# Alternating two sequences in a fused retention and feed-forward kernel, and attending two tiles in one stop

## The chip, the cores and the metric

The kernel runs on one core of a Trainium2 chip. Its time is the device time of one execution in microseconds (us); the lower, the better. The engines of the core work side by side, each on its own list of instructions in order: TensorE (PE in the profile, its weight loads PEld), VectorE (DVE), ScalarE (ACT), GpSimd (POOL) and SyncE (SP). Transfers are issued here by SyncE and GpSimd and carried out by 16 DMA engines.

## The reference

A retention layer is followed by a feed-forward layer. There are 4 sequences (batch), 8 heads, 768 tokens and 64 values a head.

```python
gamma = 1.0 - 2.0 ** (-5.0 - np.arange(H))
scale = 1.0 / np.sqrt(D)
for t in range(S):                       # attention: a decaying state for each head
    state = gamma * state + outer(k[:, :, t], v[:, :, t])
    y[:, :, t] = scale * q[:, :, t] @ state
x = y.transpose(0, 2, 1, 3).reshape(B * S, H * D)      # 3072 tokens x 512
h = x @ w_in                                           # 512 -> 2048
s = np.sin(alpha * h)
out = (h + s * s / (alpha + 1e-09)) @ w_out            # 2048 -> 512
```

## The kernel before

**Tiles and groups.** A sequence is cut into 6 chunks of 128 tokens; a chunk is a tile, numbered `j = 6 * sequence + chunk`, so there are 24. The list `order` (also `P`) is the order in which they are worked on: first chunk 0 of each of the four sequences (`e0` to `e3`), then chunks 1 to 5 of sequence 0, of sequence 1, and so on. The tiles of `order` are put together in ten groups: 4 tiles in group 0, 2 each in groups 1 to 8, 4 in group 9.

**Attention of a tile** is done in chunks: a masked product of q and k inside the tile (`scores`, then the mask on VectorE into `aT`), its product with v, the product of q with the state that earlier chunks left (`inter`, from `s_q`), and the addition of the tile's own k and v product to the state (`sums`; VectorE adds it to `s_f` in `keep`, and `hand` copies `s_f` to a bf16 `s_q`). The decay is taken into v (multiplied by `kg` or `kgq` in `scale_v`) and into the result (`leave`, which multiplies by `qg` into `xT`). One call of `burst(old, new)` makes one stop on TensorE: `inter` and the rest of the old tile, and the scores of the new one, so that VectorE can mask these until the next stop. `behind(last)` makes TensorE wait until the matmul `last` has written.

A tile has one of two forms. A *narrow* tile is loaded by itself (`load_chunk`: q and k into `qkr`, v into `vr`; for tiles in `spread`, q and k in two transfers each) and needs 16 score matmuls of 128 columns and a mask over 1024 columns. A *wide* tile (`wide(j)`) is laid out with half of its tokens on each half of the partitions, so that the upper right quarter of the scores isn't worked out: 768 columns. Wide tiles are loaded a whole sequence at a time (`load_seq`: for each of q, k, v eight transfers, one a head, each with all chunks of that head). Before, the wide ones are chunks 3 to 5 of sequence 1 and chunks 1 to 5 of sequences 2 and 3.

**Transposes.** q and k are needed with the head's values on the partitions (`qkT`). For the first tiles TensorE transposes; from `order[8]` on `turn(j)` has SyncE issue a DMA transpose (L278) two stops ahead. It waits for the loads of q and k, and what stands behind it on SyncE's list, output stores among it, waits with it.

**Feed-forward.** A phase `g` works on group `g` slot by slot: `Slot` makes the first product (L515, 8 matmuls into one bank of `ph`), ScalarE takes sine and square (L518, L523), VectorE combines both in `add` (L530) into `gT`. After each slot's matmuls stand the output matmuls (L540) of the group before, 4 in each slot of groups 2 to 8 when these have 8 slots. A stop stands behind the slot's first product: slot (g, n) is slot n of phase g.

**Where stops stand.** The stops of the two tiles of group g + 1 stand in slots 1 and 5 of phase g; the four of group 9 in slots 0, 2, 4 and 6 of phase 8. The order on every engine is that of the program, written out by hand (`manual_schedule`); waits come from the data alone.

**PSUM** has eight banks: four of tag `mm` (`ph`, output tiles `po` and others), two of `two` (`py`, the old tile's result) and two of `pa` (the new tile's scores, with the state sums of a wide tile in columns 384 to 512).

**Loads.** GpSimd issues nearly all loads, since they change float to bf16, in the order of the program, and between them it multiplies v by the decay (L158), which waits for that v. Its list behind the first tiles reads: chunk loads up to `order[10]`, then q, k, v of sequence 1, of sequence 2, of sequence 3, with products of v in between.

Of the kernel before, what the change touches and what calls it, by code (L numbers as in the profile page):

```python
# [16 lines left out]
def kernel(  # L17
# [31 lines left out]
    order += [b * NCH + c for b in range(B) for c in range(1, NCH)]  # L49
# [18 lines left out]
    raw = {}  # L68

# [8 lines left out]
    def spread(j):  # L78

        return j in order[8:11]  # L80
# [21 lines left out]

    def wide(j):
        return j >= NCH + 3 and j % NCH > 0
# [38 lines left out]
    wake = consts.tile([32, 256], F32, name="wake")  # L143
    nc.sync.dma_start(out=wake, in_=w_in_v[0:32, 0, 0:256])
    alpha_row = consts.tile([FF, 128], F32, name="alpha_row")
# [8 lines left out]
    def scale_v(j, eng):  # L154
        t, by = raw["v", j], kg
        if wide(j):
            t, by = t.rearrange("i f p d -> i (f p) d"), kgq
        eng.tensor_mul(t, t, by[:, j % NCH, :, None].to_broadcast([128, H, D]))  # L158
# [83 lines left out]
    s_f = big.tile([128, NP, D], F32, name="s_f")  # L242
    s_q = [big.tile([128, NP, D], BF16, name=f"s_q{i}") for i in range(2)]
# [3 lines left out]
    xT = {}  # L247

# [32 lines left out]
    def stage_A(j, parts=1):  # L281
# [7 lines left out]
        aT = st["aT", j] = work.tile([128, 2, NP, 128], BF16, name="aT", tag="aT", bufs=2)  # L289
# [8 lines left out]
    def first_state(j):  # L298

        ps = psum.tile([128, NP, D], F32, name="ps", tag="mm", bufs=4)  # L300
        for b, m, e in heads:
            h = head(b, m, e)
            nc.tensor.matmul(ps[half(e), 2 * b + m, :], raw["k", j][:, h, :], raw["v", j][:, h, :],
                             start=(b == 0 and m == 0), stop=True, skip_group_check=True)

        def copies():
            nc.scalar.copy(s_q[1], ps)
            nc.vector.tensor_copy(s_f, ps)
        return copies
# [27 lines left out]
    def inter(j, apart):  # L337

        qkT, s = st["qkT", j], s_q[j % NCH % 2]
# [16 lines left out]
    def scores(j):  # L356

        qkT = st["qkT", j]
        pa = st["pa", j] = psum.tile([128, 2, 512], F32, name="pa", tag="pa")
        if not wide(j):  # L360
# [4 lines left out]
            aT = st["aT", j] = work.tile([128, 2, NP, 128], BF16, name="aT", tag="aT", bufs=2)  # L365
            return {"mask": lambda: nc.vector.tensor_mul(aT.rearrange("p e n t -> p (e n) t"),  # L366
                                                         pa.rearrange("p e (n t) -> p (e n) t", n=NP), mask_bc)}
        for m in range(2):
            for b, e in tiles4:
                nc.tensor.matmul(pa[half(b), e, 192 * m:192 * m + 128].rearrange("p (f i) -> p f i", f=2),  # L370
                                 qkT[half(e), 2 + m, half(b)], qkT[half(e), m:m + 5:4, half(b)],
                                 start=(m == 0), stop=True, skip_group_check=True)
            for b, e in tiles4:
                nc.tensor.matmul(pa[half(b), e, 192 * m + 128:192 * m + 192],
                                 qkT[half(e), 6 + m, half(b)], qkT[half(e), 4 + m, half(b)],
                                 start=False, stop=True, skip_group_check=True)
        aT = st["aT", j] = work.tile([128, 2, 2, 192], BF16, name="aTw", tag="aT", bufs=2)
        return {"mask": lambda: nc.vector.tensor_mul(aT, pa[:, :, 0:384].rearrange("p e (m t) -> p e m t", m=2),  # L378
                                                     maskq[:, None, None, :].to_broadcast([128, 2, 2, 192]))}

    def sums(now, to, lo, rs=(0, 1)):

        ks, vs = raw["k", now], raw["v", now]
        for r in rs:
            for b, m, e in heads:
                if wide(now):
                    bank, at, kh, vh = b, lo, ks[half(b), r, 2 * m + e, :], vs[half(b), r, 2 * m + e, :]
                else:
                    h, f = head(b, m, e), b ^ r
                    bank, at, vh = f, lo, vs[half(f), h, :]  # L390
                    kh = ks[half(f), h, :]
                last = nc.tensor.matmul(to[bank][half(e), at + 64 * m:at + 64 * m + 64], kh, vh,  # L392
                                        start=False, stop=True, skip_group_check=True)
        return last
# [6 lines left out]
    def mix(j, tiles):  # L401

        py, aT, vs = st["py", j], st["aT", j], raw["v", j]
        for m in range(2):
            for f in range(2):
                for b, e in tiles:
# [238 lines left out]
    def phase(g, outs, att, nf=1, on_vector=()):  # L645
# [3 lines left out]
        for n in range(FF // nf):  # L649
# [6 lines left out]
            if fresh:  # L656
                rest[0] = fresh
# [179 lines left out]
```

## Time and profile before

| | before |
|---|---|
| time of the runs, median of 3 | 209.84 us (209.36 to 212.28) |
| span of the profiled execution, first to last instruction | 207.7 us |
| granted TensorE clock, mean | 1.000 |
| PE busy | 197.8 us, 95% |
| DVE busy | 151.8 us, 73% |
| ACT busy | 152.5 us, 73% |
| POOL busy | 117.6 us, 57% |
| bytes moved by DMA | 24.79 MB in 102634 packets, 93088 of them under 512 bytes |

The span is the profiled execution's own time between its first and its last instruction; the time of a run has some microseconds around it, here 2.1 between the median and the span. Busy times of one engine can be compared with the span, but not added over engines. In the rows of a timeline the first number is the start in us from the beginning of the span, the second the length. Matmuls are pipelined, so two that follow each other can overlap in these rows. "x8" is a count of instructions that the row merges, and brackets hold the idle time of the engine before it and what ended it. A name such as L515 is a line of the kernel.

### The profile page before, as it was taken

What the parts mean: (1) busy time and instruction counts of PE and PEld (TensorE: products, weight loads), DVE (VectorE), ACT (ScalarE), POOL (GpSimd) and SP (SyncE); (2) the same over time, 40 slices, a digit from 0 to 9 for tenths busy, and PEclk for the clock granted to TensorE, in tenths of its full rate; (3) what the DMA queues carried; (4) which work ended last, traced back from release to release, by engine and by line L of the source; (5) the groups of instructions that cost most, each with busy time, mean ns of one, the idle gap of its engine ahead of it and who ended that gap; (6) DMA issues with size and microseconds to landing.
All of it is one profiled execution on the core that took longest, in us unless ns stands there. A gap on an engine that the chain in (4) does not pass through costs nothing.

```text
span 207.7 us, 5741 instructions
## 1 busy us (share of the span) xinstructions
PE 197.8 (95%) x2339; PEld 123.2 (59%) x2367; DVE 151.8 (73%) x315; ACT 152.5 (73%) x311; POOL 117.6 (57%) x159
## 2 busy tenths in 40 slices
PE   7789999999999999999999999999999999999994
PEld 3345544467766676666666666666666654444453
DVE  5777498677999987868878868868888965656220
ACT  7769788457997787687687687687686779998001
POOL 8999975899999999997599910002022300000000
DMA  8999999999999999999999994421421101010212
GB/s 131 153 176 194 200 197 172 167 181 188 151 124 161 141 207 143 173 103 171 170 146 146 160 146 44 104 72 33 106 68 36 54 2 52 0 51 3 101 51 101
DMA packets 102634, 24.79 MB, mean 119 GB/s; under 512 B 93088, under 2 KB 99664, under 8 KB 102608
## 3 DMA queue, kind: packets, MB, share of 16 engines
q0 software_dynamic: 79808, 13.38, 92.2%
q1 hardware_dynamic: 22656, 10.99, 24.9%
q8 instruction: 18, 0.29, 0.6%
q10 hardware_dynamic: 144, 0.07, 0.1%
q14 instruction: 8, 0.07, 0.1%
HBM read 27.30 MB, written 6.29 MB: 162 GB/s over the span
## 4 chain that ended last, share of the span: by engine, by line
PE 83%; POOL 6%; DMA 3%; ACT 3%; issue 2%; DVE 1%; POOLq 0%
PE po L540 37%; PE ph L515 37%; DMA w_out<-in_moe_w_out_dram 3%; POOL qkr L100 3%; PE py L353 2%; POOL vr L100 2%; PE poh L565 2%; ACT s L518 2%; PE py L407 1%; ACT s L523 1%; PE pt L269 1%; PE pa L370 1%; POOL w_in L131 1%; PE pa L363 1%; PE pa L392 1%
## 5 line engine op out<-in xcount | busy, mean ns | idle before, releaser
L530 DVE SCALAR_TENSOR_TENSOR gT<-s,rec_alpha,ph 128x256 bf16<-128x256 f32 (+3 forms) x164 | 79.9, 523 | 31.5 <-ACT s L523 31.2
L515 PE MATMUL ph<-xT,w_in 128*128 128x256 bf16 (+3 forms) x652 | 98.4, 290 | 0.8 <-issue 0.3
L518 ACT ACTIVATE s<-ph,alpha_sb 128x256 f32<-128x256 f32 (+3 forms) x164 | 76.1, 507 | 27.3 <-PE ph L515 27.2
L540 PE MATMUL po<-w_out,gT 128*128 128x512 bf16 x345 | 90.7, 379 | 2.8 <-issue 2.4
L515 PEld LDWEIGHTS <-w_in 128*128 128x128 bf16 x656 | 63.3, 98 | 33.6 <-issue 0.9
L523 ACT ACTIVATE s<-s 128x512 f32<-128x512 f32 (+1 forms) x94 | 58.8, 625 | 3.0
L540 PEld LDWEIGHTS <-gT 128*128 128x128 bf16 x368 | 34.0, 98 | 30.2 <-DVE gT L530 0.5
L486 POOL CAST s_q<-s_f 128x256 bf16<-128x256 f32 x5 | 2.0, 397 | 35.5 <-DVE s_f L471 19.1
L552 DVE COPY o_sb<-po 128x512 f32<-128x512 f32 x20 | 13.8, 690 | 10.3 <-PE po L540 9.8
L120 POOL DMA_DIRECT2D qk_seq<-in_q_dram x24 | 17.0, 756 | 4.0 <-DMA v_seq<-in_v_dram 4.0
L120 POOL DMA_DIRECT2D qk_seq<-in_k_dram x24 | 16.8, 739 | 0.1
L120 POOL DMA_DIRECT2D v_seq<-in_v_dram x24 | 16.8, 752 | 0.0
L158 POOL TENSOR_TENSOR v_seq<-v_seq,kgq 128x512 bf16<-128x512 bf16 x13 | 13.6, 1071 | 4.3 <-DMA v_seq<-in_v_dram 4.3
L460 DVE TENSOR_TENSOR xT<-py,qg 128x512 bf16<-128x512 f32 x19 | 13.0, 684 | 0.6 <-PE py L423 0.6
L378 DVE TENSOR_TENSOR aTw<-pa,maskq 128x768 bf16<-128x768 f32 x13 | 12.4, 952 | 0.0
L100 POOL DMA_DIRECT2D vr<-in_v_dram x11 | 10.2, 928 | 1.0 <-DMA w_in<-in_moe_w_in_dram 0.6
L569 ACT COPY o_sb<-poh 128x256 f32<-128x256 f32 (+1 forms) x2 | 0.6, 320 | 11.7 <-PE poh L565 11.2
L585 PE MATMUL spare<-warm 128*128 128x512 bf16 x21 | 7.5, 485 | 1.2 <-DVE warm L181 1.2
L366 DVE TENSOR_TENSOR aT<-pa,mask 128x1024 bf16<-128x1024 f32 x7 | 8.5, 1219 | 0.2 <-PE pa L363 0.2
L486 ACT CAST s_q<-s_f 128x256 bf16<-128x256 f32 x14 | 5.5, 392 | 3.1 <-DVE s_f L480 2.6
L100 POOL DMA_DIRECT2D qkr<-in_k_dram x7 | 6.3, 895 | 2.2 <-DMA qkr<-in_q_dram 1.1
L100 POOL DMA_DIRECT2D qkr<-in_q_dram x7 | 6.4, 920 | 0.4 <-DMA w_out<-in_moe_w_out_dram 0.4
(106 smaller groups left out, 161.7 us busy)
## 6 DMA issues: line engine op xcount, KB each, us to landing
out_dram<-o_sb SPq DMA_DIRECT2D x23, 256.0 KB, 2.7
w_in<-in_moe_w_in_dram POOLq DMA_DIRECT2D x8, 256.0 KB, 8.1
w_out<-in_moe_w_out_dram POOLq DMA_DIRECT2D x6, 256.0 KB, 8.6
vr<-in_v_dram POOLq DMA_DIRECT2D x11, 128.0 KB, 5.9
qk_seq<-in_q_dram POOLq DMA_DIRECT2D x16, 80.0 KB, 6.2
qk_seq<-in_k_dram POOLq DMA_DIRECT2D x16, 80.0 KB, 4.8
v_seq<-in_v_dram POOLq DMA_DIRECT2D x16, 80.0 KB, 5.3
qkr<-in_q_dram POOLq DMA_DIRECT2D x7, 128.0 KB, 5.4
```

Source lines behind the costliest of these rows:

```text
L100: nc.gpsimd.dma_start(out=t, in_=chunk_of(src, j))
L120: nc.gpsimd.dma_start(out=o, in_=src[bt, head(b, m, e), cs[0] * C:, :].rearrange("(f i) d -> i f d", i=64))
L158: eng.tensor_mul(t, t, by[:, j % NCH, :, None].to_broadcast([128, H, D]))
L366: return {"mask": lambda: nc.vector.tensor_mul(aT.rearrange("p e n t -> p (e n) t"), pa.rearrange("p e (n t) -> p (e n) t", n=NP), mask_bc)}
L378: return {"mask": lambda: nc.vector.tensor_mul(aT, pa[:, :, 0:384].rearrange("p e (m t) -> p e m t", m=2), maskq[:, None, None, :].to_broa ...
L460: nc.vector.tensor_mul(o, st["pyw", old][:, :, 0:256].rearrange("p b (m t) -> p b m t", m=2), by)
L515: nc.tensor.matmul(self.ph[:, m, :], w_in[:, i, f * 128:(f + 1) * 128], xT[g][:, i, self.lo:self.hi], start=(m == 0 and i == 0), stop=(i = ...
L518: nc.scalar.activation(out=self.s[:, m, :], in_=self.ph[:, m, :], func=ACTF.Sin, scale=alpha_sb[:, f:f + 1])
L523: nc.scalar.activation(out=self.s, in_=self.s, func=ACTF.Square)
L530: nc.vector.scalar_tensor_tensor(gT[self.g][:, f, self.lo:self.hi], self.s[:, m, :], rec_alpha[:, f:f + 1], self.ph[:, m, :], op0=ALU.mult ...
L540: nc.tensor.matmul(po[g, ts], gT[g][:, f, ts * C:(ts + 1) * C], w_out[:, f, :], start=(f == 0), stop=(f == FF - 1))
L552: nc.vector.tensor_copy(o_sb, po[g, ts])
```

## The change

**Order.** Behind the first four tiles, chunks of sequences 0 and 1 take turns (chunk 1 of 0, chunk 1 of 1, chunk 2 of 0, ...), then those of sequences 2 and 3. States are kept for all four sequences in `s_f`, and two at a time in `s_q`. The state that chunk 0 leaves is worked out early for sequences 1, 2 and 3 (`first_state`), and no longer in the last stop of the sequence before.

**Forms.** Wide are now sequences 2 and 3 alone; `order[4]` to `order[13]` are narrow. q and k of `order[8]` to `order[13]` are loaded by GpSimd, half a tile at a time.

**v as float.** v of `order[8]` to `order[13]` is read by SyncE without a change of type into `vf` (three buffers), in its list beside the transposes. The product with the decay then writes it as bf16 into `vr`; GpSimd does it for `order[8]` and `order[10]`, VectorE for the four others.

**Joint stops.** From `order[14]` on, `pair(old, new)` does for both tiles of a group what `burst` did for one: `inter` of both into one `y` of two banks, the scores of the next group's first tile into `pa`, the products with v of both, then the scores of the second new tile into two `mm` banks. VectorE masks and adds the state of the first at once, of the second behind the slot's `add`. The slot after takes its `ph` from `pa`. Joint stops stand in slot 4 of phases 5, 6 and 7 and in slots 1 and 4 of phase 8. The stop of `order[13]` stands in slot 4 of phase 4 and makes the scores of both `order[14]` and `order[15]`.

**Loads of sequences.** GpSimd's list now reads: q and k of `order[8]` to `order[13]`, q of sequence 2 (`loads_a`), then k of 2, q and k of 3, v of 2, v of 3 (`loads_b`), and products of v behind.

Small parts: `aT` has three buffers, and two tiles of the start share the buffers of `s`.

```diff
     order = [b * NCH for b in range(B)]
-    order += [b * NCH + c for b in range(B) for c in range(1, NCH)]
+    order += [b * NCH + c for p in range(0, B, 2) for c in range(1, NCH) for b in (p, p + 1)]
...
-        return j in order[8:11]
+        return j in order[8:14]
...
+    def near_v(j):
+        vf[j] = work.tile([128, H, D], F32, name="vf", tag="vf", bufs=VF)
+        nc.sync.dma_start(out=vf[j], in_=chunk_of(v, j))
...
-        return j >= NCH + 3 and j % NCH > 0
+        return j >= 2 * NCH and j % NCH > 0
...
     def scale_v(j, eng):
+        if j in vf:
+            t = raw["v", j] = big.tile([128, H, D], BF16, name="vr", tag="vr", bufs=11)
+            eng.tensor_mul(t, vf.pop(j), kg[:, j % NCH, :, None].to_broadcast([128, H, D]))
+            return
...
+    def pair(old, new):
+        c, s0 = old[0] % NCH, old[0] // NCH
+        keeps = c < NCH - 1
+        y = psum.tile([128, 2, 2, 256], F32, name="y", tag="two")
+        for t, j in enumerate(old):
+            qkT, s = st["qkT", j], s_q[c % 2][:, t]
+            for b, m, e in heads:
+                o = y[half(e ^ b), e, t, m * 128:(m + 1) * 128].rearrange("p (f i) -> p f i", f=2)
+                last = nc.tensor.matmul(o, s[half(e), 2 * b + m, :], qkT[half(e), m:m + 5:4, half(b)],
+                                        start=(t == 0 and m == 0), stop=True, skip_group_check=True)
+        more = {}
+        if new is not None:
+            more.update(scores(new[0]))
+            if keeps:
+                sums(old[0], st["pb", new[0]], 384)
+        behind(last)
+        for t, j in enumerate(old):
+            mix(j, y[:, :, t])
+        if new is not None:
+            more.update(scores(new[1], "mm"))
+            if keeps:
+                sums(old[1], st["pb", new[1]], 384)
...
     stage_T(P[4], nc.vector, "pa")
+    copies = first_state(e1)
...
     stage_T(P[5], nc.scalar, "mm")
+    copies = first_state(e2, e3)
...
     load_chunk(P[10], "qk")
-    load_chunk(P[9], "v")
-    scale_v(P[8], nc.gpsimd)
-    load_seq(1, "q")
-    load_seq(1, "k")
...
+    load_chunk(P[11], "qk")
+
+    def loads_a():
+        scale_v(P[8], nc.gpsimd)
+        load_chunk(P[12], "qk")
+        load_chunk(P[13], "qk")
+        load_seq(2, "q")
+
+    def loads_b():
+        scale_v(P[10], nc.gpsimd)
+        load_seq(2, "k")
+        load_seq(3, "q")
+        load_seq(3, "k")
+        load_seq(2, "v")
+        load_seq(3, "v")
+        for j in P[14:18]:
+            scale_v(j, nc.gpsimd)
...
+    at(1, 1, 0, lambda: near_v(P[8]), X(P[8]))
+    at(1, 2, 0, B(P[6], P[7]), lambda: near_v(P[9]), X(P[9]))
+    at(1, 3, 0, loads_a)
...
+    at(1, 5, 0, B(P[7], P[8]), lambda: near_v(P[10]), X(P[10]))
+    at(1, 6, 0, loads_b)
...
+    def stop(g, n, i):
+        at(g, n, 0, BB(i))
+        do(g, n, 0, "mask", "keep0")
+        do(g, n, 1, "keep1", "mask0", "mask1")
+        do(g, n + 1, 0, "exit0")
+        do(g, n + 1, 1, "exit1", "hand")
+        tags[g][n + 1] = "pa"
+
+    for n in range(8, 14):
+        g, m = n // 2 - 2, (1 + n % 2 * 4 if n < 13 else 4)
+        at(g, m, 0, B(P[n], P[n + 1] if n < 13 else tuple(P[14:16])), X(P[n + 3]))
+        if n < 11:
+            at(g, m, 0, lambda j=P[n + 3]: near_v(j))
...
+    for g in range(5, NG - 1):
+        i = 2 * g + 4
+        stop(g, 1 if g == NG - 2 else 4, i)
+        if g < NG - 2:
+            at(g, 1, 0, X(P[i + 3]))
+        if i + 4 < NJ:
+            at(g, 5, 0, X(P[i + 4]))
...
+    at(NG - 3, 6, 0, X(P[-1]))
+    stop(NG - 2, 4, NJ - 2)
```

More of the change, by code (lines that the diff above doesn't have):

```diff
@@ L478, in keep @@
[L478 to L490 removed]
+            if not apart:
+                o, src = s_f[:, sq].rearrange("p (b m) d -> p b m d", b=2), st["pyw", old][:, :, 256:384]
+                nc.vector.tensor_add(o, o, src.rearrange("p b (m d) -> p b m d", m=2))
+                return
@@ L728 @@
     a.add()
+    copies()
     m4 = scores(P[4])["mask"]
```

273 lines of the change are left out of this document (128 added, 145 removed).

## The prediction

> **What bounds the kernel now.** I read the page first, its shares, its slices and its chain.
>
> ```profile
> span 207.7 us, 5741 instructions
> PE 197.8 (95%) x2339; PEld 123.2 (59%) x2367; DVE 151.8 (73%) x315; ACT 152.5 (73%) x311; POOL 117.6 (57%) x159
> DMA  8999999999999999999999994421421101010212
> q0 software_dynamic: 79808, 13.38, 92.2%
> PE 83%; POOL 6%; DMA 3%; ACT 3%; issue 2%; DVE 1%; POOLq 0%
> ```
>
> TensorE is busy 95% of the span and carries 83% of the chain, so an edit is worth what it takes from TensorE or makes it wait. But the DMA row is at nine tenths or more until slice 24, about 125 us. Loads and matmuls are both full there, and an edit that asks for data sooner can turn the second limit into the first. In the chain in order of time (start, length, work) the price of a stop can be read.
>
> ```profile
> 66.90 0.87 PE ph L515 x8
> ...
> 68.64 0.87 PE ph L515 x8
> ...
> 71.34 0.87 PE ph L515 x8
> ...
> 121.68 0.87 PE ph L515 x8
> ...
> 123.42 0.87 PE ph L515 x8
> ...
> 125.97 0.87 PE ph L515 x8
> ```
>
> Two slots of a group lie 1.74 us apart (66.90 to 68.64). With a stop of a narrow tile it is 2.70 (to 71.34), with a wide one 2.55 (123.42 to 125.97): a narrow stop costs 0.96 us, a wide one 0.81. From TensorE's timeline, the matmuls of slot 4 of group 4, which matter below, and a wide stop from the slot before it on:
>
> ```profile
> 98.08 1.04 PE L515 MATMUL ph<-xT,w_in 128*128 128x256 bf16 x8
> ...
> 123.25 1.04 PE L515 MATMUL ph<-xT,w_in 128*128 128x256 bf16 x8
> 124.22 0.31 PE L353 MATMUL py<-qkT,s_q 64*64 64x128 bf16 x8
> ...
> 124.53 0.30 PE L392 MATMUL pa<-v_seq,qk_seq 64*64 64x64 bf16 x16
> 124.66 0.34 PE L407 MATMUL py<-aTw,v_seq 64*64 64x128 bf16 x16
> ```
>
> The slot's last matmul would be followed at 123.25 + 0.87 = 124.12; the stop begins at 124.22, so 0.10 is lost on entry. State sums take 0.13 (124.53 to 124.66).
>
> **The change, part by part.** *Joint stops.* Ten one-tile stops (order[14] to order[23]) become five. Matmuls are kept; an entry and an exit go per pair. The entry is 0.10. The exit is not shown alone: from 124.66 the stop has until 124.12 + 0.81 = 124.93, 0.27 for 16 matmuls, the like of which (the 16 scores and 16 sums) take 0.13 to 0.18, so 0.1 to 0.14 of it is exit. I take 0.24 a pair, bounds 0.10 to 0.28: −1.2 us (−0.5 to −1.4).
>
> *Other TensorE work.* Three tiles of sequence 1 (order[11] to order[13] in the new order) become narrow: 3 × 0.15 = +0.45. Sums fall from 19 stops to 16, −0.39. Three first states are made early, 24 matmuls of the form below, 8 of which were 0.3 us with their pipeline tails: +0.45, half that to twice 0.45 as bounds.
>
> ```profile
> L303 PE MATMUL ps<-vr,kb 128*64 128x64 bf16 x8 | 0.3, 195 | 0.0
> ```
>
> Together with the joint stops −0.7 us.
>
> *Banks and VectorE.* The slot after a joint stop takes its accumulator from the pair of banks that the mask and the first state sum must leave. In VectorE's timeline of the stop at 124.12:
>
> ```profile
> 124.13 0.87 DVE L530 SCALAR_TENSOR_TENSOR gT<-s,rec_alpha,ph 128x256 bf16<-128x256 f32 x2 [0.86 <-ACT s L523]
> 124.92 0.95 DVE L378 TENSOR_TENSOR aTw<-pa,maskq 128x768 bf16<-128x768 f32 x1
> ...
> 127.25 0.41 DVE L480 TENSOR_TENSOR s_f<-s_f,pa 128x256 f32<-128x256 f32 x1
> ```
>
> Mask ends at 125.87, the sum (now directly behind it) at 126.3: 2.2 us after the stop begins. TensorE comes there after a joint stop of 2 × 0.81 − 0.24 = 1.38 and four output matmuls, 0.87: 2.25. That hides it, by 0.05 us. Cost zero, bounds 0 to 0.3 × 4. The two masks and one more sum of the second tile wait behind, with a slot and a half of room. The extra v products on VectorE are two more than before, in groups with slack, and cost nothing; the longer copies on GpSimd or ScalarE have two slots until the next joint stop. A third aT buffer and two start-up tiles that share the buffers of s cost nothing: the tiles are long done when a slot wants their place.
>
> *The float v loads.* They join SyncE's queue beside the transposes of the same tiles, the first behind the third store:
>
> ```profile
> 44.63 1.27 SPq L555 DMA_DIRECT2D out_dram<-o_sb  x2
> ```
>
> ```profile
> o_sb<-in_q_dram SPq DMA_DIRECT2D x1, 256.0 KB, 3.3
> ```
>
> Such a load of q took 3.3 us at the start. Issued at 45.9, order[8]'s v is there by 49 to 51, and GpSimd comes to its product 16 half loads and two products after 42.28, near 57: no wait, and none for the transposes behind, unless the load takes over 11 us.
>
> *The loads of whole sequences, the large term.* In the old order the first tile of sequence 3 is order[19], wanted at its stop in group 7; now the chunks of sequences 2 and 3 alternate, so order[15] is sequence 3's, and its scores stand in slot 4 of group 4, ahead of the first joint stop. Its transpose on SyncE waits for all sixteen q and k transfers of sequence 3, since each head brings all chunks. GpSimd's timeline and the DMA issues of a stretch (count, KB each, median us to landing) show what they need:
>
> ```profile
> 42.28 1.52 POOL L98 DMA_DIRECT2D qkr<-in_q_dram  x2
> ...
> 45.25 1.11 POOL L158 TENSOR_TENSOR vr<-vr,kg 128x512 bf16<-128x512 bf16 x1
> ...
> 73.02 4.39 POOL L120 DMA_DIRECT2D qk_seq<-in_q_dram  x6
> ...
> 101.55 1.43 POOL L120 DMA_DIRECT2D qk_seq<-in_q_dram  x2 [1.74 <-DMA v_seq<-in_v_dram]
> 102.99 3.04 POOL L158 TENSOR_TENSOR v_seq<-v_seq,kgq 128x512 bf16<-128x512 bf16 x3
> ```
>
> ```profile
> qk_seq<-in_q_dram POOLq DMA_DIRECT2D x16, 80.0 KB, 6.2
> out_dram<-o_sb SPq DMA_DIRECT2D x4, 256.0 KB, 4.8
> qk_seq<-in_k_dram POOLq DMA_DIRECT2D x8, 80.0 KB, 4.5
> v_seq<-in_v_dram POOLq DMA_DIRECT2D x8, 80.0 KB, 6.1
> qkT<-qk_seq SPq DMA_TRANSPOSE x4, 7.4
> ```
>
> ```profile
> qk_seq<-in_q_dram POOLq DMA_DIRECT2D x2, 80.0 KB, 6.3
> ```
>
> Before, q, k and v of sequence 2 and q of sequence 3 are 32 transfers of 80 KB. The first is issued at 73.02; the last two, issued from 101.55 on, land about 6.3 later, the very last near 108.4. So 32 transfers, with four transposes and four stores between, took 35.4 us, 1.1 each. That is not GpSimd's issuing: it waited for earlier v transfers to land (1.74 in the row of 101.55).
>
> After, the 32 that must land first are q and k of both sequences. GpSimd still starts order[8]'s loads at 42.28. By 0.76 an issue (1.52 for two) it has 24 half loads for six tiles, 18.2, and three products of 1.1: the first transfer of sequence 2 goes at 42.28 + 21.5 = 63.8. The 32 then end at 99.2. Added are the float v loads of three tiles in that stretch: 1024 rows of 64 values each, against 640 in an 80 KB transfer, hence 1.6 × 1.1 = 1.8 us each if they cost the same a row, 5.3, and 0 if they fit beside. Taken away are the times of before when the queue ran dry while GpSimd multiplied inside this stretch: three products of 1.1 (1.11 in the row of 45.25), some of it covered by queued transfers; I put it at 2 us (bounds 0 and 3.3). I take 3 for the v loads, so +1 net: the last k lands at 100.2, bounds 95.9 and 104.5. The transpose behind it, with v transfers still queued as at 90 to 100 us, has these landings (min, median, max):
>
> ```profile
> DMA to landing us min/median/max: 5.9/7.1/9.3
> ```
>
> So order[15] is transposed at 107.3, from 101.8 to 113.8. TensorE wants it at 98.08 + 0.87 for the slot, + 0.4 into the stop (ahead of it come the old tile's first round and the scores of order[14]), + 0.5 for the first states and narrow tiles so far: 99.8. TensorE takes its work in order, so **it stands for 7.5 us**, bounds 2.0 and 14.0, with the feed-forward slots behind it and, behind those, ScalarE and VectorE. Nothing gives this back, since TensorE is full to the end. On SyncE's queue two stores and the transposes of order[16] and on stand behind this wait; an output tile has three buffers, and those tiles are wanted a group later.
>
> A quicker landing is possible: if the transpose took turns with the queued v transfers rather than follow them, it would land like the quickest of all sixteen, 3.0 us in the next row; the wait would be 100.2 + 3.0 − 99.8 = 3.4 and the time 207.7 − 0.7 + 3.4 + 1.8 + 2.1 = 214.3, the 1.8 being the next term.
>
> ```profile
> DMA to landing us min/median/max: 3.0/5.3/9.3
> ```
>
> The Trainium skill (DMA: Bandwidth & Descriptors, Queues, rings and completion order) says that a DMA engine takes turns between the queue rows that have work, packet by packet. The 5.9 to 9.3 above disagree, so I keep 7.1.
>
> *TensorE's speed after it has stood.* Only the start shows it:
>
> ```profile
> 1.19 3.95 PE L585 MATMUL spare<-warm 128*128 128x512 bf16 x9 [1.19 <-DVE warm L181]
> ...
> 12.41 0.82 PE L585 MATMUL spare<-warm 128*128 128x512 bf16 x3
> ```
>
> Nine matmuls take 3.95 us, less a tail of some 0.17 (0.82 for three that issue at 0.22), 0.42 each, later 0.22: 1.8 us lost. Before has no other such idle time; the bounds are 0 and 1.8, and I take 1.8, the only row of a TensorE that comes from rest. The Trainium skill (TensorE: Matmul & The Clock Gate, Part 1: The HAM clock gate) states a half clock after an idle window of about 3.4 us until as long a busy one; by it the loss would be an estimated 1.7 us.
>
> **The sum.** 207.7 − 0.7 + 7.5 + 1.8 = 216.3 us of span. The median of the runs, 209.84, is 2.1 above the profiled span, and I carry that along: **218.4 us**. Its own range: 207.7 − 0.7 + 2.0 + 0 + 2.1 = 211.1, and 207.7 − 0.7 + 14.0 + 1.8 + 2.1 = 224.9.
>
> **Rivals.** *The loads come in time (not slower).* If the q and k of sequence 3 land by 92.7 (99.8 less 7.1), no wait arises and the PE terms alone remain: 209.84 − 0.7 = 209.1 us. For it: GpSimd alone, at 0.73 an issue (4.39 for six), would be through at 63.8 + 24 = 88, and much v work is off its queue. Against it: the same 32 transfers would have to take 29 us with more beside them, where they took 35.4 with the DMA row full.
>
> *A second wait (slower still).* The v of sequence 3 is last in the queue. Before, all loads had landed only here:
>
> ```profile
> 123.73 1.04 POOL L158 TENSOR_TENSOR v_seq<-v_seq,kgq 128x512 bf16<-128x512 bf16 x1 [4.29 <-DMA v_seq<-in_v_dram]
> ```
>
> The joint stop in slot 4 of group 5 wants that v scaled. It comes eight slots (13.9) and a stop (about 1.0) after 107.3, at 122.2; with landing at 123.7, a product of 1.1 and 0.6 into the stop, (123.7 + 1.1 − 122.8) 2 us are added: 220.4, and 227 with the first wait at its upper bound. For it: as many rows as before. Against: no pauses of the queue for products.
>
> *The joint stop loses.* If banks make TensorE wait 0.3 us at four stops, then on-time loads give 210.3: nothing that could be told.
>
> **Chances.** The first wait 0.72 (0.10 of it with turns taken, 214.3), loads in time 0.16 (the bank waits in it), the second wait 0.12. 210 to 225 leaves out the in-time case and the far end of the second wait: 0.8 inside. Within 2% (about what a measurement of this kernel can tell from no change) is 205.6 to 214.0: the in-time case, and of the first the part with a wait up to 3 us, 0.09. Faster by more than 2% would need 4.2 us, and TensorE idles little more than that while groups run, 82 − 79.91 = 2.1 us from 42 to 124:
>
> ```profile
> 42.00:124.00 82.00, 79.91 (x1169) 56.10 (x1170) 66.95 (x136) 65.03 (x139) 73.48 (x100) 1.00 1.92 157
> ```
>
> So 0.02 faster, 0.25 same, 0.73 slower.
>
> **What would show it.** Right: one idle time of TensorE, 2 to 14 us, at about 99.8 before the scores of the second tile in group 4, released by the transpose; SyncE waiting for k of sequence 3; slow matmuls right after; joint stops of 1.3 to 1.4 us later. Wrong: no wait over 2 us in that slot, the k landed before 93, or joint stops followed by idle time on VectorE's masks.

## The result, and the profile after

| | before | after |
|---|---|---|
| median of the runs | 209.62 us (209.36 to 212.28) | 218.47 us (217.41 to 221.4) |
| span of the profiled execution | 207.7 us | 216.7 us |
| granted TensorE clock, mean | 1.000 | 0.976 |

The table of before counts four runs here, one more than ahead of the prediction. Here and below, medians are of all runs, while a ratio and its interval leave out runs that lie over 1.5% above the fastest of the same kernel, and compare with runs of the kernel before that were taken beside them. The change makes the kernel slower: 1.0367 of the time before, 95% interval 1.0279 to 1.0454. The prediction was 218.4. The page of the profile after, in the order of the lines that were shown of before:

```profile
span 216.7 us, 5756 instructions
...
PE 203.0 (94%) x2343; PEld 124.9 (58%) x2343; DVE 153.1 (71%) x321; ACT 152.3 (70%) x309; POOL 105.7 (49%) x140
...
PE   7889999999999999994199999999999999999994
...
PEclk9999999999999999999569999999999999999999
DMA  9999999999999999999994266133241101010212
...
PE 49%; DMA 24%; POOL 23%; issue 2%; DVE 0%; SPq 0%; POOLq 0%
```

TensorE's share of busy time hardly moved (95% to 94%), so that figure would not give the change away. Three others do. The PE row has a hole in slices 18 and 19 (digits 4 and 1), about 98 to 108 us. The clock row falls to 5 and 6 in the two slices around the end of the hole. And the chain, which was 83% TensorE, is now 49%: before the hole it no longer runs through TensorE but through loads and the GpSimd that issues them. TensorE's timeline around the hole:

```profile
98.44 1.04 PE L554 MATMUL ph<-xT,w_in 128*128 128x256 bf16 x8
...
99.76 0.24 PE L395 MATMUL pa<-qkT 64*64 64x64 bf16 x4
107.59 0.32 PE L391 MATMUL pb<-qkT 64*64 64x128 bf16 x4 [7.59 <-DMA qkT<-qk_seq]
...
108.27 1.89 PE L579 MATMUL po<-w_out,gT 128*128 128x512 bf16 x4
109.95 1.91 PE L554 MATMUL ph<-xT,w_in 128*128 128x256 bf16 x8
111.66 1.45 PE L579 MATMUL po<-w_out,gT 128*128 128x512 bf16 x4
112.94 1.04 PE L554 MATMUL ph<-xT,w_in 128*128 128x256 bf16 x8
```

In slot 4 of group 4 the scores of order[14] are done (99.76), and those of order[15] stand for 7.59 us until the transpose of its q and k has landed. Behind that the matmuls are slow: three groups that take 0.87 each elsewhere need 112.94 − 108.27 = 4.67, so 2.06 are lost. The rest of the stop itself, from 107.59 to 108.27, takes 0.68; where TensorE had rested only 1.59 us (the last experiment) it takes 0.41, so 0.27 more. Together 2.3 us.

SyncE's timeline has the issue of that transpose, SyncE's waits have what its line (L291) waited for (in total, how often, longest), and the view of that line from 100 to 104 us has the time to landing:

```profile
102.76 1.25 SPq L291 DMA_TRANSPOSE qkT<-qk_seq  x1
```

```profile
SPq L291 <- DMA qk_seq<-in_k_dram: 15.7, 2, 9.6
```

```profile
DMA to landing us min/median/max: 4.8/4.8/4.8
```

The longer of its two waits for k, 9.6 us, ended just ahead of 102.76 and was for sequence 3. GpSimd's timeline has the loads ahead of the transpose, from the first of the 32 to the last, and the v products of sequence 2 and 3 behind:

```profile
62.84 0.73 POOL L128 DMA_DIRECT2D qk_seq<-in_q_dram  x1 [0.41 <-DMA qkr<-in_q_dram]
...
70.00 0.71 POOL L128 DMA_DIRECT2D qk_seq<-in_q_dram  x1 [1.94 <-DMA qkr<-in_q_dram]
...
97.49 0.72 POOL L128 DMA_DIRECT2D qk_seq<-in_k_dram  x1 [0.72 <-DMA qk_seq<-in_q_dram]
...
116.47 4.04 POOL L170 TENSOR_TENSOR v_seq<-v_seq,kgq 128x512 bf16<-128x512 bf16 x4 [4.87 <-DMA v_seq<-in_v_dram]
```

The balance of the two profiled spans: 216.7 − 207.7 = 9.0 = 7.6 (the wait) + 2.3 (slow matmuls) − 0.9 (what is left for TensorE's own work, not measured by itself here).

Two joint stops on TensorE, each from the slot before it to the output matmuls behind it, and VectorE's share of the first:

```profile
123.36 1.04 PE L554 MATMUL ph<-xT,w_in 128*128 128x256 bf16 x8
...
125.75 1.04 PE L579 MATMUL po<-w_out,gT 128*128 128x512 bf16 x4
126.62 1.04 PE L554 MATMUL ph<-xT,w_in 128*128 128x256 bf16 x8
...
138.78 1.04 PE L554 MATMUL ph<-xT,w_in 128*128 128x256 bf16 x8
...
141.04 1.04 PE L579 MATMUL po<-w_out,gT 128*128 128x512 bf16 x4
```

```profile
125.11 0.96 DVE L400 TENSOR_TENSOR aTw<-pa,maskq 128x768 bf16<-128x768 f32 x1
125.98 0.41 DVE L514 TENSOR_TENSOR s_f<-s_f,pa 128x256 f32<-128x256 f32 x1
```

The second lasts from 138.78 + 0.87 = 139.65 to 141.04: 1.39 us for two tiles. The first takes 125.75 − 124.23 = 1.52. Behind it the next slot (126.62) starts 0.87 after the output matmuls, so it does not wait for its bank.

### The profile page after: what moved, and what is told of

Read it like the earlier page. It is cut to its first block, busy times and chain, and to the rows that moved or that the text cites. A ratio compares the mean times of both kernels' runs of the same rounds, so it can differ in the third digit from the quotient of the medians.

```text
span 216.7 us, 5756 instructions
## 1 busy us (share of the span) xinstructions
PE 203.0 (94%) x2343; PEld 124.9 (58%) x2343; DVE 153.1 (71%) x321; ACT 152.3 (70%) x309; POOL 105.7 (49%) x140
## 4 chain that ended last, share of the span: by engine, by line
PE 49%; DMA 24%; POOL 23%; issue 2%; DVE 0%; SPq 0%; POOLq 0%
PE po L579 23%; PE ph L554 21%; DMA qk_seq<-in_k_dram 7%; POOL qkr L99 6%; DMA qkr<-in_q_dram 4%; DMA qk_seq<-in_q_dram 4%; DMA vr<-in_v_dram 4%; POOL qkr L101 4%; POOL w_in L139 3%; POOL qg L246 2%; DMA qkT<-qk_seq 2%; POOL vr L101 2%; POOL w_out L143 2%; PE poh L604 2%; POOL vr L170 1%
## 5 line engine op out<-in xcount | busy, mean ns | idle before, releaser
L579 PE MATMUL po<-w_out,gT 128*128 128x512 bf16 x368 | 96.6, 383 | 0.1
L128 POOL DMA_DIRECT2D qk_seq<-in_q_dram x16 | 11.4, 718 | 8.2 <-DMA qkr<-in_q_dram 4.0
L128 POOL DMA_DIRECT2D qk_seq<-in_k_dram x16 | 11.5, 747 | 3.7 <-DMA qk_seq<-in_q_dram 3.7
L170 POOL TENSOR_TENSOR v_seq<-v_seq,kgq 128x512 bf16<-128x512 bf16 x10 | 10.4, 1057 | 4.9 <-DMA v_seq<-in_v_dram 4.9
L387 DVE TENSOR_TENSOR aT<-pa,mask 128x1024 bf16<-128x1024 f32 x10 | 12.2, 1219 | 0.0
L128 POOL DMA_DIRECT2D v_seq<-in_v_dram x16 | 11.4, 780 | 0.9 <-DMA qk_seq<-in_k_dram 0.7
L402 DVE TENSOR_TENSOR aTw<-pb,maskq 128x384 bf16<-128x384 f32 x10 | 5.1, 550 | 6.2 <-PE pb L395 6.2
L99 POOL DMA_DIRECT2D qkr<-in_q_dram x12 | 9.3, 791 | 0.0
L99 POOL DMA_DIRECT2D qkr<-in_k_dram x12 | 9.2, 793 | 0.0
L447 DVE TENSOR_TENSOR xT<-y,qg 128x512 bf16<-128x512 f32 x10 | 6.8, 682 | 0.0
```

The source lines that it names most:

```text
L99: nc.gpsimd.dma_start(out=t[:, NP * o:NP * o + NP], in_=chunk_of(src, j)[:, o::2])
L128: nc.gpsimd.dma_start(out=o, in_=src[bt, head(b, m, e), cs[0] * C:, :].rearrange("(f i) d -> i f d", i=64))
L579: nc.tensor.matmul(po[g, ts], gT[g][:, f, ts * C:(ts + 1) * C], w_out[:, f, :], start=(f == 0), stop=(f == FF - 1))
```

## The experiments

**Is it the loads of q and k, and which of them?** The theory is the prediction's: the transpose of order[15] waits for the last k of sequence 3, which stands behind too much in a full queue. Five edits follow: one lets the transpose read data that is there, the others move, thin out or cut what is queued ahead of it.

*The tile's transpose reads a tile that is there* (p15_near); order[15] is then computed from q and k of order[14]:

```diff
-        nc.sync.dma_start_transpose(out=st["qkT", j], in_=raw["qk", j].rearrange(
+        at = order[14] if j == order[15] else j
+        nc.sync.dma_start_transpose(out=st["qkT", j], in_=raw["qk", at].rearrange(
```

> The changed kernel, but the transpose of order[15] reads q and k of order[14] (sequence 2) in place of its own, so it need not wait for sequence 3; that tile is computed from the wrong q and k. Every load stays where it is. Theory, the late load of sequence 3: the 7.6 us in which TensorE stood before the second tile's scores go, and with them some 2.4 us of slow matmuls behind it; span 216.7 - 10.0 = 206.7. v of order[15] was multiplied by 117.5 and would now be wanted near 115.6, so up to 2 us may come back at the first joint stop: 206.7 to 208.7 of span, 208.5 to 210.5 of time. Rival, the joint stops and the alternating order cost by themselves: the time stays over 214.

Measured: 216.08 us, four runs from 212.38 to 218.52, too wide for an interval. The run of 212.38 had a mean granted clock of 0.999, the three others 0.984 to 0.992. SyncE's and TensorE's timelines:

```profile
93.94 2.48 SPq L292 DMA_TRANSPOSE qkT<-qk_seq  x1
```

```profile
104.24 0.32 PE L392 MATMUL pb<-qkT 64*64 64x128 bf16 x4 [3.58 <-DMA qkT<-qk_seq]
...
123.12 0.37 PE L425 MATMUL y<-aTw,v_seq 64*64 64x128 bf16 x16 [1.00 <-POOL v_seq L170]
```

The expectation was missed. The transpose went out at 93.94, 8.8 us earlier than after the change, and TensorE still stood 3.58 us for it, until 104.24: it landed 10.3 us after its issue. So a transpose whose data is there can be late as well, when it is issued while the loads are queued. It also had SyncE's own work ahead of it, the transpose of order[14] issued at 91.88, which took 7.8 us to land, and a store issued at 93.22; this run does not tell which of the two queues held it up. The v of sequence 3, the second wait among the rivals, shows up here with 1.00 us, once the first has shrunk. Half of the wait was left, so this run does not show alone that k is the cause.

*v of sequence 2 ahead of q and k of sequence 3* (v2_ahead):

```diff
+        load_seq(2, "v")
         load_seq(3, "q")
         load_seq(3, "k")
-        load_seq(2, "v")
```

> The changed kernel with the eight v transfers of sequence 2 issued ahead of q and k of sequence 3. Theory, TensorE waits for a full DMA: 32 transfers took from 62.8 to 102.4 in the changed kernel, 1.24 each, so eight more put the last k of sequence 3 at 112.3 and the wait at 17.5 us; the time is 228.4, the slow matmuls cost the same. If GpSimd's issuing were the limit, eight issues of 0.72 add 5.8: 224.2. Rival, the wait is for the transpose's own queue (stores and transposes on SyncE), not the loads: 218.5 as before.

Measured: 223.74 us, ratio to before 1.0653 (1.058 to 1.0727). SyncE's and TensorE's timelines:

```profile
107.44 1.25 SPq L291 DMA_TRANSPOSE qkT<-qk_seq  x1
```

```profile
112.49 0.32 PE L391 MATMUL pb<-qkT 64*64 64x128 bf16 x4 [12.16 <-DMA qkT<-qk_seq]
```

Eight transfers more in front put the transpose off by 107.44 − 102.76 = 4.7 us, the wait up by 12.16 − 7.59 = 4.6 and the time up by 5.3. That the order of the queue sets the time is shown; the rival (no change) falls. The forecast of 228.4 was missed: one added transfer cost 0.6 us, half of the 1.24 that the theory took. The time lies next to the 224.2 that stood for a limit by GpSimd's issuing, so this run does not part that from a full DMA. Two things speak against GpSimd: on the page of after it sits idle for 8.2 us ahead of the sixteen q and 3.7 us ahead of the sixteen k, until earlier transfers have landed, and pool_v below adds six issues to its list without the 5.4 us that this limit would have added.

*Three float v loads less* (three_v):

```diff
+        if j in order[11:14]:
+            vf[j] = vf[order[order.index(j) - 3]]
+            return
         vf[j] = work.tile([128, H, D], F32, name="vf", tag="vf", bufs=VF)
...
-            eng.tensor_mul(t, vf.pop(j), kg[:, j % NCH, :, None].to_broadcast([128, H, D]))
+            eng.tensor_mul(t, vf[j], kg[:, j % NCH, :, None].to_broadcast([128, H, D]))
```

> The changed kernel without the float loads of v of order[11] to order[13]; their products read v of order[8] to order[10] instead, so those three tiles are computed from the wrong v. Theory, these loads take DMA time ahead of sequence 3's k, about 1.0 us each as I had put them: the last k lands 3 us earlier, the wait is 4.6, the time 215.5; between 213.1 (1.8 each) and 218.5 (none, if they fit beside).

Measured: 216.21 us, ratio 1.0287 (1.0222 to 1.0351). SyncE's and TensorE's timelines:

```profile
99.70 1.26 SPq L294 DMA_TRANSPOSE qkT<-qk_seq  x1
```

```profile
104.75 0.32 PE L394 MATMUL pb<-qkT 64*64 64x128 bf16 x4 [3.94 <-DMA qkT<-qk_seq]
```

The transpose goes out 3.06 us earlier and the wait shrinks by 3.65, which fits the 3 us that the prediction put down for these loads. This compares one profile of each kernel, and under an unchanged list of loads the same transpose went out anywhere from 102.76 to 105.09 (kept_warm and kept_warm38 below); the intervals of the two ratios overlap. So the 3 us are supported, not shown.

*v by GpSimd as bf16 again* (pool_v): the six tiles' v goes back into GpSimd's list, each ahead of the next q or k.

```diff
     def near_v(j):
-        vf[j] = work.tile([128, H, D], F32, name="vf", tag="vf", bufs=VF)
-        nc.sync.dma_start(out=vf[j], in_=chunk_of(v, j))
+        pass
...
     load_chunk(P[9], "qk")
+    load_chunk(P[8], "v")
...
         load_seq(2, "q")
 
     def loads_b():
         scale_v(P[10], nc.gpsimd)
+        load_chunk(P[13], "v")
         load_seq(2, "k")
```

> The changed kernel with v of order[8] to order[13] loaded by GpSimd as bf16, as before, each next to q and k of the tiles around it, in place of the float loads on SyncE. Theory, the DMA is full and the rows are the same: 218 to 219, within 1 us of the changed kernel. If GpSimd's issuing were the limit, six issues of 0.9 would add 5.4: 224. If the float form were the dear part (twice the bytes written): 3 to 5 us less, 214 to 215.

Measured: 216.43 us, ratio 1.0302 (1.0248 to 1.0356). SyncE's and TensorE's timelines:

```profile
100.87 1.24 SPq L290 DMA_TRANSPOSE qkT<-qk_seq  x1
```

```profile
105.33 0.32 PE L390 MATMUL pb<-qkT 64*64 64x128 bf16 x4 [5.05 <-DMA qkT<-qk_seq]
```

Six more loads stand on GpSimd's list, and yet the transpose goes out 1.9 us earlier. With GpSimd's issuing as the limit, 224 was expected; that falls. The theory's own forecast, 218 to 219, was missed as well: the median lies 2.0 us below the change as made. The intervals of the two ratios overlap (1.0248 to 1.0356 and 1.0279 to 1.0454), so it is not shown that reading v as float costs anything by itself; if it does, it is some 2 of the 9 us.

*Only what is needed first* (split_loads): the loads of sequences 2 and 3 are cut in two, chunks 1 to 3 first, chunks 4 and 5 of sequence 2 behind them, those of sequence 3 with all later v only in phase 6.

```diff
-    def load_seq(bt, names="qkv"):
+    def load_seq(bt, names="qkv", part=0):
...
-        cs = [c for c in range(NCH) if wide(bt * NCH + c)]
+        cs = ((1, 2, 3), (4, 5))[part]
...
+        load_seq(2, "q", 1)
+        load_seq(2, "k", 1)
+
+    def loads_c():
+        load_seq(3, "q", 1)
+        load_seq(3, "k", 1)
+        load_seq(2, "v", 1)
+        load_seq(3, "v", 1)
...
+    at(6, 0, 0, loads_c)
```

> The changed kernel with the loads of sequences 2 and 3 cut in two: chunks 1 to 3 of both (q, k of 2 and 3, then v of both) at the place of before, chunks 4 and 5 behind them, half of these issued in phase 6; one copy of the states goes from GpSimd to ScalarE. Nothing of the result changes. Theory, the order of the loads alone makes the wait: ahead of the first joint stop are 12288 rows in place of 20480, the k of sequence 3 lands near 93 and its transpose near 98, before TensorE asks at 99.8; the wait and the slow matmuls go, span 206.7, time 208.5, 0.5 to 1% under the kernel before. If a transpose takes up to 10 us in the full queue, as it did in one run, 2 to 5 us of wait stay: 211 to 214. Rival, alternating and joint stops cost by themselves: not under 210.4.

Measured: 209.99 us, ratio 1.0006 (0.9969 to 1.0044); clock 1.000, span 207.8. SyncE's and TensorE's timelines:

```profile
96.43 1.24 SPq L291 DMA_TRANSPOSE qkT<-qk_seq  x1
```

```profile
99.80 1.04 PE L554 MATMUL ph<-xT,w_in 128*128 128x256 bf16 x8
...
101.12 0.20 PE L395 MATMUL pa<-qkT 64*64 64x64 bf16 x2
101.14 0.23 PE L391 MATMUL pb<-qkT 64*64 64x128 bf16 x2
```

The scores of order[15] (101.14) follow those of order[14] without a gap. Order, joint stops and float v are all kept (one copy of a state goes from GpSimd to ScalarE beside the cut loads), and 8.5 us are gone: the wait and the slow matmuls behind it. By the ratios, each to its own runs of before, it is 7.6 us. That is the cause, shown on the whole kernel. The small gain over before that was expected (208.5) is not there; this execution began the product above at 99.80, where the change as made had it at 98.44, and the section on the prediction comes back to that.

**What would the change be worth without its loads?** In seq3_from_2 sequence 3 is not loaded at all; its tiles are computed from sequence 2, and its products of v are left out:

```diff
...
-        load_seq(3, "q")
-        load_seq(3, "k")
         load_seq(2, "v")
-        load_seq(3, "v")
+        for j in range(3 * NCH + 1, 4 * NCH):
+            for name in ("qk", "k", "v"):
+                raw[name, j] = raw[name, j - NCH]
```

> The changed kernel in which sequence 3 is not loaded: its chunks 1 to 5 are computed from q, k and v of sequence 2, already in place, and its products of v are left out. Everything that TensorE, VectorE and ScalarE do is kept. Theory: no wait for loads is left, and TensorE's own terms show alone, -0.7 against the kernel before with bounds -1.4 and +0.3: 208.9 beside 209.6. Rival, banks or masks hold TensorE at the joint stops: 210 to 211.

Measured: 209.4 us, ratio 0.9979 (0.9947 to 1.001), 0.4 us faster with an interval of −1.1 to +0.2. Joint stops, fewer sums and early states together are worth between nothing and 1 us; the predicted 0.7 fits, and so does no gain.

**Do the matmuls behind the wait really cost 2 us?** The first try put spare matmuls into the wait, so that TensorE should not rest (kept_warm with 30, kept_warm38 with 38):

```diff
         if tail is not None:
+            keep_on = psum.tile([128, 512], F32, name="keep_on", tag="mm", bufs=4)
+            for _ in range(30):
+                nc.tensor.matmul(keep_on, warm[:, :128], warm, start=True, stop=True)
             more.update(scores(tail, "mm"))
```

> The changed kernel with 30 spare matmuls of 512 columns (6.5 us at full speed) on TensorE between the scores of order[14] and of order[15], where it stood for 7.6. Theory, TensorE is slow behind the wait because it had stood: the matmuls behind it run at 0.22 us from the first, the wait's end stays at 107.6, and 2.0 to 2.4 us are saved: 216.1 to 216.5. Rival, they are slow for another reason (DMA, waits of ScalarE or VectorE that had fallen behind): 218.5.

> As the run with 30 spare matmuls, but 38 (8.2 us), since the wait had outlived the 30 by 3.1 us in the profile and the matmuls behind it were slow again. Theory, slow because it had stood: TensorE stands for under 2 us, the matmuls behind run at full speed, granted clock 1.000, and the time is 216 to 217; where the wait is shorter than 8.2 us, up to 1 us of that is spent on spare work. Rival: 218.5 to 219.

Measured: 219.02 us, ratio 1.0306 (1.0217 to 1.0396), and 218.58 us, ratio 1.0434 (1.0369 to 1.05). Neither saved anything that can be told from the change as made. In kept_warm two runs with a mean granted clock of 1.000 took 216.03 and 217.58, near the 216.1 to 216.5 that were expected, and two with 0.992 took 220.47 (the profiled one) and 220.55. TensorE's timelines, first kept_warm, then kept_warm38, tell why:

```profile
110.28 0.25 PE L391 MATMUL pb<-qkT 64*64 64x128 bf16 x4 [3.10 <-DMA qkT<-qk_seq]
```

```profile
100.15 8.38 PE L461 MATMUL keep_on<-warm 128*128 128x512 bf16 x38
110.97 0.25 PE L391 MATMUL pb<-qkT 64*64 64x128 bf16 x4 [2.45 <-DMA qkT<-qk_seq]
...
111.38 1.56 PE L582 MATMUL po<-w_out,gT 128*128 128x512 bf16 x4
112.73 1.92 PE L557 MATMUL ph<-xT,w_in 128*128 128x256 bf16 x8
```

The loads came later in these two executions (the transpose went out at 104.67 and 105.09, not 102.76), the spare work ran out, and a rest of 3.10 or 2.45 us was left, with slow matmuls behind it all the same. The question stayed open, so the rest was made by hand, in split_loads and in its last phase, where nothing else waits: TensorE waits for six GpSimd products (stand6) or two (stand2), or does 30 spare matmuls beside the same six products (work6). The edit below is stand6's. In work6 the last loop has 30 turns and its matmul reads `warm` in place of `chain[1]`; in stand2 the first loop has one turn.

```diff
+    def rest():
+        nc.gpsimd.tensor_mul(chain[0], gT[NG - 1][:, 3, :], warm)
+        for i in range(5):
+            nc.gpsimd.tensor_mul(chain[1 - i % 2], chain[i % 2], warm)
+        out = psum.tile([128, 2, 512], F32, name="rest", tag="two")
+        for _ in range(1):
+            nc.tensor.matmul(out[:, 0], warm[:, :128], chain[1], start=True, stop=True)
+
+    at(NG - 1, 4, 0, rest)
```

> The split_loads kernel (no wait on TensorE, 209.99 us) with a rest put in by hand in the last phase: behind the first product of its fifth slot stands one spare matmul that needs the last of six GpSimd products of 128x512 in a row, the first of which reads the slot before. At 1.04 us each (GpSimd's rows in split_loads) they take 6.3 us, and TensorE stands S of 6.3 to 7.5 us. Nothing else is on GpSimd then. Theory (a TensorE that has stood runs its next matmuls at half speed for a while, 2.0 to 2.4 us lost, as in the rows behind the wait of the changed kernel): 210.0 + S + 2.2, near 219, with matmuls of twice the length behind the rest. Rival (those rows were slow for another reason, DMA traffic or operands that came late, or the loss is taken back later): 210.0 + S, near 217, with no slow rows.

> The same kernel with the same six GpSimd products, but TensorE doesn't need them: in their place it does 30 spare matmuls of 512 columns, 30 x 0.216 = 6.5 us of work. Both theories: 210.0 + 6.5 = 216.5 us. The difference of stand6 to this run, less (S - 6.5), is what the rest costs beyond its own length: 2.2 us by the theory, 0 by the rival.

> The same with two GpSimd products in place of six: TensorE stands 2.1 to 3.3 us. If any rest slows the next matmuls: 210.0 + 2.7 + 2.2 = 214.9. If only a long rest does (the wait of 2.45 us in kept_warm38 had slow rows behind it, so a short one may do): 210.0 + 2.7 = 212.7, with no slow rows.

Measured: stand6 219.81 us, ratio 1.0476 (1.0435 to 1.0517); work6 215.14 us, 1.0247 (1.021 to 1.0284); stand2 214.29 us, 1.0184 (1.0144 to 1.0225). TensorE's timelines, first stand6, then work6, then stand2:

```profile
173.77 1.03 PE L554 MATMUL ph<-xT,w_in 128*128 128x512 bf16 x4
183.10 0.59 PE L890 MATMUL rest<-chain,warm 128*128 128x512 bf16 x1 [8.30 <-POOL chain L887]
183.47 1.06 PE L579 MATMUL po<-w_out,gT 128*128 128x512 bf16 x2
184.33 1.91 PE L554 MATMUL ph<-xT,w_in 128*128 128x512 bf16 x4
...
188.44 1.03 PE L554 MATMUL ph<-xT,w_in 128*128 128x512 bf16 x4
```

```profile
174.56 6.64 PE L890 MATMUL rest<-warm 128*128 128x512 bf16 x30
181.03 0.59 PE L579 MATMUL po<-w_out,gT 128*128 128x512 bf16 x2
...
184.06 1.03 PE L554 MATMUL ph<-xT,w_in 128*128 128x512 bf16 x4
```

```profile
180.00 0.38 PE L890 MATMUL rest<-chain,warm 128*128 128x512 bf16 x1 [3.39 <-POOL chain L887]
180.21 0.59 PE L579 MATMUL po<-w_out,gT 128*128 128x512 bf16 x2
180.64 1.03 PE L554 MATMUL ph<-xT,w_in 128*128 128x512 bf16 x4
```

Between the end of the slot's product and the next output matmuls, stand6 has 183.47 − 174.64 = 8.83 us (174.64 is 173.77 + 0.87) and work6 181.03 − 174.56 = 6.47; that is 2.36 of the difference. The medians differ by 4.67. The 2.3 that are left are the price of having rested. The rows, of one profile each, give a little less: from the first output matmuls to the product of the third slot after, 188.44 − 183.47 = 4.97 in stand6 and 184.06 − 181.03 = 3.03 in work6, 1.9 more. The rival, that those rows were slow for another reason, would have no difference left; it falls, since in this last phase no loads were under way and the rows show no other wait. stand6 lies above its 219 because the rest came out at 8.30 in place of up to 7.5; work6 lies 1.4 below the 216.5. Its profile shows that this arose ahead of the edit: the product in slot 4 of group 4, which split_loads began at 99.80, began 1.55 earlier here, though the two kernels are the same up to that place.

```profile
98.25 1.04 PE L554 MATMUL ph<-xT,w_in 128*128 128x256 bf16 x8
```

In stand2's profile a rest of 3.39 us has no slow matmuls behind it. But the mean granted clock of its other runs was 0.992 in three that took 214.23 to 214.51, 0.984 in one of 219.74, and 1.000 in one of 212.36. So a rest of this length seems to slow TensorE in some executions; no profile shows it there.

**Is there a faster version?** split_pool joins the two edits that helped, split_loads and pool_v (their diffs stand above).

> split_loads with v of order[8] to order[13] loaded by GpSimd as bf16, as in pool_v. Theory (once no transfer is waited for, a lighter load list is worth nothing; the ceiling is seq3_from_2 with 0.998 of before): 209.4 to 210.2, no gain. Rival (the transfers still cost the early part of the kernel, where pool_v saved 2 us): 208.0 to 208.7, faster than before by some 0.7%.

Measured: 210.15 us, ratio 0.9983 (0.9938 to 1.0028). TensorE's timeline:

```profile
101.55 0.25 PE L390 MATMUL pb<-qkT 64*64 64x128 bf16 x4 [1.59 <-DMA qkT<-qk_seq]
...
101.96 1.04 PE L578 MATMUL po<-w_out,gT 128*128 128x512 bf16 x4
```

No gain that can be told, as the theory had it: where the loads are cut, making them lighter as well gained nothing that these runs can tell. In this profile a short wait is even left, 1.59 us, with full-speed matmuls behind it. No version measured here beats the kernel before.

## Why the prediction was right, step by step

**The place and the kind of the wait** were right: one stand, ahead of the scores of the second tile in slot 4 of group 4, released by the transpose. It began at 107.59 − 7.59 = 100.00 (99.8 predicted) and lasted 7.59 (7.5). split_loads shows that it and its consequence are the whole loss, to within 0.9 us.

**Its size came out of two terms that were each off by 2.3 us**, in opposite directions. That 7.5 met 7.59 is luck; the working was good to some 2 us. The last k was put at 100.2; SyncE could issue only at 102.76, so it landed just short of that, near 102.5. The 32 transfers took 39.7 us from 62.84, 1.24 each, where 36.4 from 63.8 had been worked out. Of the two corrections to the old 35.4, the +3 for the float v fits three_v (3.06); the −2 for times when the queue ran dry fits nothing here: 39.7 − 35.4 = 4.3 leaves +1.3 beside the 3. GpSimd's rows from 62.84 to 70.00 offer a reason: at the start of the 32 it waits for chunk loads (qkr) that it had issued before and that hadn't landed. The prediction let the 32 begin with an empty queue; there was a backlog. That is read from the rows and was not tried by itself.

**The landing of the transpose** was put at 7.1, from stretches with full queues, and was 4.8, below the shortest of those (5.9). The rival, that a transpose takes turns with the loads and lands in 3.0, did not come about either: p15_near's needed 10.3, v2_ahead's up to 112.49 − 107.44 = 5.1, pool_v's at most 105.33 − 100.87 = 4.5. A single number for it was too much; these runs show about 4.5 to 10.3. The Trainium skill (DMA: Bandwidth & Descriptors, Queues, rings and completion order) has a DMA engine take turns between queue rows packet by packet. Neither these landings nor the 5.9 to 9.3 that the prediction read decide whether turns were taken: none here was as short as 3.0, but taking turns need not mean that nothing is lost to the other row, and the 10.3 had a transpose and a store of SyncE ahead of it too.

**Slow matmuls after the stand**: 1.8 predicted from the start of the kernel, 2.3 by the rows of after, 1.9 by the rows and 2.3 by the medians of stand6 and work6. The mechanism was right, the size a little too small. The price hardly depends on the length of the rest. Counted from the first output matmuls behind the rest to the first product of usual length, 1.7 us are lost behind 2.45 (kept_warm38) and 3.10 (kept_warm), 2.3 behind 3.58 (p15_near), 2.1 behind 3.94 (three_v) and 7.59 (after), 2.0 behind 5.05 (pool_v), 1.9 behind 8.30 (stand6) and 12.16 (v2_ahead); nothing behind 1.59 (split_pool) and 3.39 (stand2). The Trainium skill (TensorE: Matmul & The Clock Gate, Part 1: The HAM clock gate) gives half speed after an idle window of about 3.4 us, the window running freely. Full speed after 1.59 us, half speed after 8.30, and rests near 3.4 of either kind (3.39 and 3.58) agree with that. Half speed behind the 2.45 us of kept_warm38 does not, if a whole window has to be idle.

**TensorE's own terms**: −0.7 predicted. The balance of the spans leaves −0.9, seq3_from_2 has −0.4 (−1.1 to +0.2), split_loads +0.1 (−0.7 to +0.9). So the net is small, and by the medians it stays open whether it is a gain. The rows say more. From the product in slot 4 of group 4 to the end of the span, before took 207.7 − 98.08 = 109.6 us. split_loads took 207.8 − 99.80 = 108.0, and work6 212.9 − 98.25 less its 6.47 of spare work, 108.2. So behind that slot the change saves 1.4 to 1.6 us, close to the 1.2 of the joint stops and the 0.39 of the sums together; the rows do not say how much each gives. Ahead of it nothing is saved: the thirteen profiles of the new order, after and the twelve experiments, begin that product at 98.13 to 100.15, the one of before at 98.08. The prediction had allowed 0.5 for that. The start itself varies between executions: split_loads, stand2, work6 and stand6 are the same program up to there and begin at 99.80, 98.13, 98.25 and 98.43. A late start hides the gain, as in split_loads's profile; why it varies stays open. A joint stop was put at 1.38 and took 1.39 (the first 1.52).

**Banks and VectorE** cost nothing, as put down: no idle time behind a joint stop. VectorE's mask and sum of the first one end at 126.39; the next slot's product started at 126.62.

**The rivals.** The loads did not come in time. The second wait for v did not come: the products at 116.47 were done by 120.5, ahead of the joint stop that began at 124.23. In p15_near, where TensorE got there sooner, it came with 1.00 us, so it was real and hidden behind the first.

## What to carry to other kernels

When an order of work is changed, ask for each tile when its last byte is asked for, and price the queue ahead of that byte by what it took before, with the backlog at its start; an engine's busy share won't show the danger (95% and 94% here). Where transfers bring several tiles at once, a new order makes the whole transfer due at its earliest tile: cutting the transfers into what is needed first and what is needed later took back all of the loss. And a wait on TensorE cost about 2 us more than its own length in every profile here in which it was 3.58 us or longer.

## What was not expected of the hardware

- Added transfers of 80 KB cost 0.6 us each (v2_ahead), while the same list took 1.24 each on average; the mean price of a transfer in a mixed queue is not the price of one more.
- The same list of loads gave different times for the last k: its transpose went out at 102.76 in after, 104.67 in kept_warm and 105.09 in kept_warm38, although nothing ahead of it differs.
- A transpose of data that had landed took 10.3 us while loads were queued, with another transpose and a store of SyncE ahead of it (p15_near).
- Rests of 2.45 and 3.10 us had slow matmuls behind them in one profile each, a rest of 3.39 us had none: length alone does not decide there. The eight rests with slow matmuls behind them, of 2.45 to 12.16 us, cost 1.7 to 2.3 us beyond their length, the longest no more than the others.
